# A fused convolution and feed-forward kernel: how its first block is evicted and transposed, and which engine copies the weights' exchanged halves

## The chip, the cores and the metric

The kernel runs on one core of a Trainium2 chip. The metric is the device time of one execution in microseconds (us); less is better. The median of three runs before the change is 536.28 us (536.27 to 536.34).

A core has a matrix engine (PE, with its weight loads shown as PEld), a vector engine (DVE), a scalar engine (ACT), a general engine that also issues the casting loads (POOL, GpSimd) and a queue engine for other transfers (SP). PE writes its results to PSUM. Here PSUM is used as four slots of two banks each, handed out in rotation under one tag, "banks".

## The reference

```python
w = softmax(weight, axis=-1)                     # 8 heads x 7 taps
x_pad = concatenate([zeros(B, 6, D), x], axis=1) # B, S, D = 8, 3904, 192
out[b, s, h, g] = sum_k w[h, k] * x_pad[b, s + k, h, g]   # 8 heads of 24 channels
x = out.reshape(31232, 192)
a = x @ w1                                       # 192 -> 1024
b = x @ w2                                       # 192 -> 1024
return ((a * b) @ w3) @ w_out                    # 1024 -> 1024 -> 192
```

## The kernel before, in words

**Two streams.** The 31232 tokens are cut into two halves (streams r = 0 and 1) of 15616 tokens that are worked on together. The partitions 64r to 64r+63 belong to stream r wherever an operand has 64 channels in 128 partitions.

**Convolution.** A window is 64 tokens, of which 58 give results. Windows are grouped in blocks of 10, 8, 10, 18, 16, 20, 36 ... windows (`SIZES`). `load_x` loads a block's windows as bf16; `conv(b, h0, nh)` (L240 to L269) multiplies them with a small band matrix per head (`Aband`, L203 to L224, made from the taps) into the PSUM tile `cps`, and L266 evicts that to the block's tile `convo`, in pieces of at most 64 channels. The channel groups k = 0, 1, 2 are channels 0 to 63, 64 to 127 and 128 to 191; four heads are 96 channels, so the first half of a block fills group 0 and half of group 1 and the second half the rest.

**Transposes.** The products want channels on partitions. For the first three blocks `pe_transposes` (L298 to L313) does it on PE: all groups go to one PSUM tile `tps` (five transposes each for block 0), and L311 copies each group to `xT[k]`, a ring of 2048 tokens. Later blocks go through DRAM (`store`, `transposes`).

**Products.** `first_product(R)` (L339 to L362) handles 512 tokens of each stream. For each of eight column groups ft of 128 columns it makes `pa` (x @ w1) and `pb` (x @ w2): six matmuls each, in pairs r = 0, 1 over k = 0, 1, 2. ACT evicts `pa` to `asb` (L358), DVE multiplies `asb` with `pb` into `abT` (L359). `second_product` (L364) multiplies `abT` with `W_sb` = w3 @ w_out, which is itself made during the first rounds by `fold` (w3 is transposed on PE at L401 and multiplied at L410).

**The weights' exchanged halves.** A matmul of stream r contracts over the 64 partitions 64r to 64r+63, so both streams need each weight on both halves of the partitions. `wn[0]` holds w1's channels 0 to 127, `wn[1]` those of w2, and `wn[2]` holds w1's channels 128 to 191 in partitions 0 to 63 and w2's in partitions 64 to 127. `wsw[k]` is `wn[k]` with its two halves of 64 partitions exchanged. `swap_w` (L328 to L331) makes it with two copies, one for each half, and the column half (512 columns) is an argument; the list of engines names who does which copy. `w_of` (L323) says which tile a matmul takes: `pa` needs `wsw[0]` and one half of `wsw[2]`, `pb` needs `wsw[1]` and the other half of `wsw[2]`. A column group ft needs the columns 128 ft to 128 ft + 127.

**Order of the work.** It is written out by hand: each engine does its instructions in the order of the program. Around the change that order is: warm-up matmuls on zeros (`warm`, L175 to L178: five, then the matmul that spreads the taps, then seven), the band, `load_x(1)`, the two convolutions of block 0 with evictions by (ACT, DVE) and (DVE, ACT), its 15 transposes, the copies to `xT` (DVE, ACT, DVE) with the exchange of `wsw[0]`'s columns 0 to 511 after the first, then the other exchanges of these columns, then `wsw[0]`'s upper columns by POOL. The other upper columns are exchanged inside the first product: `wsw[2]` after ft 1 and `wsw[1]` after ft 2, where the later loads are issued too. `first_product` takes a table of such insertions, done after the ft of their key: the blocks 1 and 2 are convolved and transposed there.

**POOL's loads.** POOL issues the loads in program order: block 0, the eight pieces of the weights, block 1, block 2, w_out, w3. In the trace they use eight semaphores in turn (104 to 111), and a load waits, before it is issued, for the landing of the load eight places ahead of it.

Of the kernel before, what the change touches and what calls it, by code (L numbers as in the profile page):

```python
# [16 lines left out]
def kernel(  # L17
# [10 lines left out]
    nc = tc.nc  # L28
# [4 lines left out]
    DFF = moe_w1.shape[1]  # L33
# [10 lines left out]
    ST = Q - PAD  # L44
# [4 lines left out]
    SIZES = [10, 8, 10, 18, 16, 20] + [36] * 5 + [10]  # L49
# [5 lines left out]
    def tok(i):  # L55
        return (i // WB) * S + (i % WB) * ST
# [8 lines left out]
    def banks(name):  # L65
        return psum.tile([128, NS, CH], FP32, tag="banks", name=name)

    def banks_bf16(name):
        return psum.tile([128, 16, 128], BF16, tag="banks", name=name)
# [7 lines left out]
    def halves_of(b):  # L77
        n = SIZES[b] // 2
        return [(FIRST[b], 2 * n)] if 2 * n <= MAXN else [(FIRST[b], n), (FIRST[b] + n, n)]
# [4 lines left out]
    def x_spans(r, i, m):  # L84
        return bass.AP(tensor=x.tensor, offset=(r * TS + tok(i) - PAD) * D,
                       ap=[[D, Q], [ST * D, m], [1, D]])

    def load_x(b, parts=(0, 1)):
        tiles = xb_of.setdefault(b, [])
        zeros_of = zero_rows.setdefault(b, [])  # L90
        for i0, n in [v for e, v in enumerate(halves_of(b)) if e in parts]:
            xb = work.tile([128, n, D], BF16, tag="xb", bufs=6, name="xb")
            w = 0
            if i0 == 0:
                nc.vector.memset(xb[:, 0, :], 0.0)
                for r in range(NS):
                    nc.gpsimd.dma_start(out=xb[Q * r:Q * r + Q, 1:n, :], in_=x_spans(r, 1, n - 1))  # L97
                w = n
            while w < n:
                i = i0 + w  # L100
                m = min(n - w, WB - i % WB)
                at_end = i + m == NWIN
                if at_end:
                    m -= 1
                if m:
                    for r in range(NS):
                        nc.gpsimd.dma_start(out=xb[Q * r:Q * r + Q, w:w + m, :],  # L107
                                            in_=x_spans(r, i, m))
                if i % WB == 0:
                    zeros_of += [(xb, 0, w), (xb, 1, w)]  # L110
                w += m
                if at_end:
                    nc.gpsimd.memset(xb[Q:128, w, :], 0.0)
                    t = tok(NWIN - 1) - PAD
                    nc.gpsimd.dma_start(out=xb[0:Q, w, :], in_=x_rows[t:t + Q, :])
                    nc.gpsimd.dma_start(out=xb[Q:Q + PAD + LAST, w, :],
                                        in_=x_rows[TS + t:TS + t + PAD + LAST, :])
                    w += 1
            if len(halves_of(b)) == 1:
                tiles += [(xb, 0), (xb, SIZES[b] // 2)]  # L120
            else:
                tiles.append((xb, 0))
# [13 lines left out]
    for r in range(NS):  # L136
        ps = slice(Q * r, Q * r + Q)
        nc.gpsimd.affine_select(
            out=diag[ps], in_=diag[ps], pattern=[[-1, Q + K - 1]], compare_op=ALU.is_equal,
# [11 lines left out]
    ident = const.tile([128, 128], BF16)  # L151
# [11 lines left out]
    HC = DFF // 2  # L163
# [11 lines left out]
    def warm(n):  # L175
        t = banks("warm")
        for j in range(n):
            nc.tensor.matmul(t[:, j % 2, :], zeros[:, 0:128], zeros, start=True, stop=True)  # L178

    warm(5)  # L180

    low = const.tile([H, 1], FP32)
    total = const.tile([H, 1], FP32)
# [5 lines left out]
        out=share, in0=taps.unsqueeze(1).to_broadcast([H, H, K]), scalar=total,  # L189
# [5 lines left out]
    for r in range(NS):  # L195
        ps = slice(Q * r, Q * r + Q)
        nc.vector.tensor_copy(
            out=wsb[ps],
            in_=spread[ps, 0, 0:H * K].rearrange("p (g a e k) -> p g a e k", g=2, a=2, e=2)
                [:, :, r].unsqueeze(4).to_broadcast([Q, 2, 2, K, 2]))  # L200
    warm(7)

    Aband = const.tile([128, 2, 2, 2, Q], BF16)  # L203

    def band_of(h, r):
        g, j, e = h // 4, (h % 4) // 2, h % 2
        return Aband[Q * r:Q * r + Q, g, int(j != r), e, :]
# [3 lines left out]
        out=cprod.rearrange("p h k (s two) -> p h k s two", two=2),  # L211
# [15 lines left out]
    xT = [const.tile([128, RING], BF16, name=f"xT{k}", tag=f"xT{k}") for k in range(NP)]  # L227

    convo_of = {}
    wt = {}  # L230

    def segments(c0, n):
        out = []
        while n:
            m = min(n, Q - c0 % Q)
            out.append((c0 // Q, c0 % Q, m))
            c0, n = c0 + m, n - m
        return out

    def conv(b, h0, nh, evict=None):  # L240
        n = SIZES[b] // 2
        if h0 == 0:
            convo_of[b] = work.tile([128, n, NP, NS, Q], BF16, tag="convo", bufs=2, name="convo")
        convo = convo_of[b]
        cps = banks("cps")
        wd = nh * G

        def view(ps, r):
            return cps[ps, r, 0:n * wd].rearrange("p (w g) -> p w g", g=wd)

        for j in range(nh):
            h = h0 + j
            for c in range(2):
                xb, w0 = xb_of[b][c]
                for r in range(NS):
                    nc.tensor.matmul(  # L256
                        view(slice(Q * c, Q * c + Q), r)[:, :, j * G:(j + 1) * G],
                        band_of(h, r),
                        xb[Q * r:Q * r + Q, w0:w0 + n, h * G:(h + 1) * G],
                        start=True, stop=True)  # L260
        src = cps[:, :, 0:n * wd].rearrange("p r (w g) -> p r w g", g=wd)
        o = 0
        for e, (k, c0, m) in enumerate(segments(h0 * G, wd)):
            dst = convo[:, :, k, :, c0:c0 + m].rearrange("p w r g -> p r w g")
            f = evict or [nc.scalar.copy]
            f[e % len(f)](out=dst, in_=src[:, :, :, o:o + m])  # L266
            o += m
        if h0 + nh == H:
            del xb_of[b]  # L269
# [25 lines left out]
                    nc.sync.dma_start(out=dst[s0:s1], in_=src[s0:s1])  # L295
                w += m

    def pe_transposes(b, after_first=None):  # L298
        n = SIZES[b] // 2
        convo = convo_of[b]  # L300
        tps = banks_bf16("tps")
        for k in range(NP):
            for w in range(n):
                nc.tensor.transpose(  # L304
                    out=tps[:, k * n + w, :],
                    in_=convo[:, w, k].rearrange("p r g -> p (r g)"), identity=ident)
        t0 = tok(FIRST[b])
        for k in range(NP):
            dst = xT[k][:, t0:t0 + 2 * n * ST].rearrange("p (c w s) -> p c w s", c=2, w=n)
            src = tps[:, k * n:(k + 1) * n, :].rearrange("p w (c s) -> p c w s", c=2)  # L310
            (nc.scalar.copy if k == 1 else nc.vector.tensor_copy)(out=dst, in_=src[:, :, :, 0:ST])  # L311
            if k == 0 and after_first:
                after_first()  # L313

    def transposes(R, first=0):
        t0, t1 = max(R * CH, first), min((R + 1) * CH, TS)
# [8 lines left out]
            return (wn if i == r else wsw)[2]  # L325
        return (wn if k == r else wsw)[i]

    def swap_w(k, half, engines):  # L328
        cs = slice(half * HC, (half + 1) * HC)
        for f, (d, e) in zip(engines, ((0, Q), (Q, 0))):  # L330
            f(out=wsw[k][d:d + Q, cs], in_=wn[k][e:e + Q, cs])  # L331

# [57 lines left out]
    def load_wo():  # L390
        nc.gpsimd.dma_start(out=wo_b, in_=wor)

    def load_w3(jt):
        w3b_of[jt] = stage.tile([128, DFF], BF16, tag="w3b", bufs=JT, name="w3b")
        nc.gpsimd.dma_start(out=w3b_of[jt], in_=w3r[:, jt, :])
# [19 lines left out]
    V, A, P = nc.vector.tensor_copy, nc.scalar.copy, nc.gpsimd.tensor_copy  # L415

    load_x(1)
    conv(0, 0, 4, evict=(A, V))
    conv(0, 4, 4, evict=(V, A))
    pe_transposes(0, lambda: swap_w(0, 0, (V, V)))  # L420
    swap_w(2, 0, (A, V))
    swap_w(1, 0, (A, V))
    swap_w(0, 1, (P, P))
    def seq(*fs):
        def run():
            for f, *a in fs:
                f(*a)
        return run
# [5 lines left out]
            w3_product(jt - 1)  # L434

    def later_loads():
        swap_w(1, 1, (P, V))
        load_x(2)
        load_wo()
        for jt in range(4):  # L440
            load_w3(jt)
        load_x(3)
        for jt in range(4, JT):
            load_w3(jt)
        for b in (4, 5, 6):
            load_x(b)

    first_product(0, {
        1: seq((swap_w, 2, 1, (V, A))),
        2: later_loads,  # L450
        4: seq((conv, 1, 0, 4)),
        5: seq((conv, 1, 4, 4)),
        6: seq((pe_transposes, 1)),
        7: seq((conv, 2, 0, 4))})
    first_product(1, {
        0: seq((conv, 2, 4, 4)),
        1: seq((fold, 0)),
        2: seq((pe_transposes, 2), (store, 2, 26)),
        3: seq((fold, 1)),
        5: seq((fold, 2)),  # L460
# [85 lines left out]
```

## Time and profile before

| | |
|---|---|
| median of three runs | 536.28 us |
| the profiled execution | 535.81 us |
| its span, first to last instruction | 534.1 us |
| PE busy | 523.2 us, 98% |
| DVE busy | 350.5 us, 66% |
| ACT busy | 324.0 us, 61% |
| POOL busy | 47.9 us, 9% |
| mean granted clock of PE | 0.994 |

All times of views are counted from the span's start. A line of the timeline gives start, duration, engine, line of the program, operation, tiles written and read, shape and count, and in brackets how long the engine had been idle and what released it. The stretches' table gives busy time per engine in a stretch, with the number of instructions, then the granted clock as a share of full speed. The chain of waits is followed back from the last instruction. In the trace six matmuls of a `pa` or `pb` take 0.65 us at full clock (six starts from 16.99 to 17.64 us) and twice that at half clock (13.99 to 15.28 us).

### The profile page before, as it was taken

Reading aid. Unit: us, or ns where it says so; the run is one execution under the profiler, and the core shown is the slowest. Engines: PE = TensorE matmul, PEld = TensorE weight load, DVE = VectorE, ACT = ScalarE, POOL = GpSimd, SP = SyncE. Lnnn points to the kernel's source line nnn. Section 1 sums busy time; section 2 is a strip of 40 time slices with the busy share of each in tenths; the row PEclk is TensorE's granted clock in tenths of the full one; section 3 lists DMA queues with packets and bytes.
Section 4 is the critical chain, followed back from the end, with each engine's and each line's share of the span. In section 5 each row is a group of like instructions: output and inputs, shape, how many; then the busy total and the mean of one; then the engine's idle time right before and its main releaser. Section 6 shows DMA issues by size and latency. Waiting matters only on the chain.

```text
span 534.1 us, 12779 instructions
## 1 busy us (share of the span) xinstructions
PE 523.2 (98%) x5495; PEld 345.9 (65%) x5495; DVE 350.5 (66%) x339; ACT 324.0 (61%) x368; POOL 47.9 (9%) x85
## 2 busy tenths in 40 slices
PE   6999999999999999999999999999999999999996
PEld 2445675766758567585675857658576684856676
DVE  6667639578394884939749396593956929377470
ACT  3766557566474665737657375573756647475562
POOL 8641001001010010200101010020000000000000
PEclk8899999999999999999999999999999999999999
DMA  8999568765489455974659656593316543130304
GB/s 112 165 201 192 94 141 159 125 167 68 136 154 139 119 67 155 139 148 101 83 159 146 135 90 98 156 149 112 68 35 186 79 136 75 60 104 14 108 1 149
DMA packets 130459, 63.10 MB, mean 118 GB/s; under 512 B 83270, under 2 KB 129378, under 8 KB 130402
## 3 DMA queue, kind: packets, MB, share of 16 engines
q1 hardware_dynamic: 91842, 45.65, 35.5%
q0 software_dynamic: 38544, 16.63, 25.7%
q8 instruction: 43, 0.70, 0.5%
q14 instruction: 14, 0.11, 0.1%
q10 hardware_dynamic: 16, 0.00, 0.0%
HBM read 33.25 MB, written 34.82 MB: 127 GB/s over the span
## 4 chain that ended last, share of the span: by engine, by line
PE 93%; DVE 2%; ACT 2%; DMA 1%; issue 1%; POOL 0%; ACTq 0%; POOLq 0%
PE ops L370 31%; PE pa L352 29%; PE pb L352 29%; PE cps L256 3%; DVE abT L359 2%; ACT asb L358 2%; PE wps L410 1%; DMA xb<-in_x_dram 1%; PE w3ps L401 1%; POOL xb L97 0%; DVE ws L331 0%; PE tps L304 0%; ACT convo L266 0%; DVE xT L311 0%; DVE convo L266 0%
## 5 line engine op out<-in xcount | busy, mean ns | idle before, releaser
L359 DVE TENSOR_TENSOR abT<-asb,pb 128x1024 bf16<-128x1024 bf16 (+1 forms) x248 | 298.1, 1203 | 56.2 <-ACT asb L358 38.8
L358 ACT CAST asb<-pa 128x1024 bf16<-128x1024 f32 (+1 forms) x248 | 247.6, 999 | 71.5 <-PE pa L352 70.8
L352 PE MATMUL pb<-xT,wn 64*128 64x512 bf16 (+1 forms) x744 | 202.6, 374 | 0.5
L352 PE MATMUL pa<-xT,wn 64*128 64x512 bf16 (+1 forms) x744 | 198.7, 374 | 1.3 <-DVE xT L311 1.0
L352 PE MATMUL pa<-xT,ws 64*128 64x512 bf16 (+1 forms) x744 | 198.7, 375 | 0.6 <-DVE ws L331 0.6
L352 PE MATMUL pb<-xT,ws 64*128 64x512 bf16 (+1 forms) x744 | 194.1, 374 | 0.0
L352 PEld LDWEIGHTS <-wn 64*128 64x128 bf16 x1488 | 137.4, 94 | 81.0 <-issue 6.3
L352 PEld LDWEIGHTS <-ws 64*128 64x128 bf16 x1488 | 128.2, 94 | 72.1 <-issue 4.8
L370 PE MATMUL ops<-W_sb,abT 128*128 128x192 bf16 x1952 | 166.3, 246 | 0.0
L370 PEld LDWEIGHTS <-abT 128*128 128x128 bf16 x1952 | 159.6, 98 | 9.9 <-issue 9.5
L375 ACT COPY osb<-ops 128x768 f32<-128x768 f32 (+1 forms) x62 | 48.9, 788 | 117.0 <-PE ops L370 117.0
L266 DVE CAST convo<-cps 128x864 bf16<-128x864 f32 (+10 forms) x47 | 38.3, 850 | 105.8 <-PE cps L256 104.1
L107 POOL DMA_DIRECT2D xb<-in_x_dram x36 | 28.8, 808 | 12.7 <-DMA xb<-in_x_dram 4.3
L499 POOL COPY pace<-abT 1x2 bf16<-1x2 bf16 x9 | 1.6, 174 | 269.9 <-DVE abT L359 269.9
L266 ACT CAST convo<-cps 128x864 bf16<-128x864 f32 (+9 forms) x39 | 22.3, 611 | 2.3 <-PE cps L256 1.4
L256 PE MATMUL cps<-xb,Aband 64*64 64x432 bf16 (+5 forms) x384 | 18.1, 285 | 1.3 <-DMA xb<-in_x_dram 1.0
L256 PEld LDWEIGHTS <-Aband 64*64 64x64 bf16 x384 | 6.9, 105 | 9.3 <-issue 7.7
L410 PE MATMUL wps<-wo_b,w3T 128*128 128x192 bf16 x64 | 6.6, 246 | 0.3 <-DVE xT L311 0.3
L178 PE MATMUL warm<-zeros 128*128 128x512 bf16 x12 | 4.9, 576 | 1.3 <-DVE zeros L142 1.3
L401 PEld LDWEIGHTS <-w3b 128*128 128x128 bf16 x64 | 3.9, 97 | 3.4 <-issue 3.0
L412 ACT CAST W_sb<-wps 128x192 bf16<-128x192 f32 x8 | 2.6, 319 | 5.8 <-PE wps L410 5.8
L410 PEld LDWEIGHTS <-w3T 128*128 128x128 bf16 x64 | 5.2, 98 | 0.9 <-issue 0.5
(50 smaller groups left out, 53.7 us busy)
## 6 DMA issues: line engine op xcount, KB each, us to landing
out_dram<-osb SPq DMA_DIRECT2D x60, 384.0 KB
xb<-in_x_dram POOLq DMA_DIRECT2D x20, 432.0 KB, 7.4
rows<-convo SPq DMA_DIRECT2D x8, 648.0 KB
w3b<-in_moe_w_dram POOLq DMA_DIRECT2D x8, 256.0 KB, 10.9
xb<-in_x_dram POOLq DMA_DIRECT2D x4, 336.0 KB, 9.7
xT<-rows SPq DMA_TRANSPOSE x84
rows<-convo SPq DMA_DIRECT2D x8, 135.0 KB
xb<-in_x_dram POOLq DMA_DIRECT2D x4, 216.0 KB, 4.4
```

The source lines that it names most:

```text
L107: nc.gpsimd.dma_start(out=xb[Q * r:Q * r + Q, w:w + m, :], in_=x_spans(r, i, m))
L178: nc.tensor.matmul(t[:, j % 2, :], zeros[:, 0:128], zeros, start=True, stop=True)
L256: nc.tensor.matmul(view(slice(Q * c, Q * c + Q), r)[:, :, j * G:(j + 1) * G], band_of(h, r), xb[Q * r:Q * r + Q, w0:w0 + n, h * G:(h + 1) ...
L266: f[e % len(f)](out=dst, in_=src[:, :, :, o:o + m])
L352: nc.tensor.matmul(p[:, r, 0:N], w_of(i, k, r)[rs, ft * 128:(ft + 1) * 128], xT[k][rs, r0:r0 + N], start=(k == 0), stop=(k == NP - 1))
L358: nc.scalar.copy(out=asb[:, :, 0:N], in_=pa[:, :, 0:N])
L359: nc.vector.tensor_tensor(out=ab[:, ft, :, 0:N], in0=asb[:, :, 0:N], in1=pb[:, :, 0:N], op=ALU.mult)
L370: nc.tensor.matmul(ops[:, g // 2, (g % 2) * D:(g % 2) * D + D], ab[:, jt, r, g * 128:(g + 1) * 128], W_sb[:, jt, :], start=(jt == 0), stop ...
L375: nc.scalar.copy(out=osb.rearrange("p (a g) d -> p a (g d)", g=2), in_=ops[:, 0:ng // 2, 0:2 * D])
L401: nc.tensor.transpose(out=tps[:, gt, :], in_=w3b[:, gt * 128:(gt + 1) * 128], identity=ident)
L410: nc.tensor.matmul(wps[:, 0, 0:D], w3T[:, gt, :], wo_b[:, gt, :], start=(gt == 0), stop=(gt == JT - 1))
L412: nc.scalar.copy(out=W_sb[:, jt, :], in_=wps[:, 0, 0:D])
```

## The change

Four things change, all at the start of the kernel:

- block 0's first convolution tile is evicted by ACT alone, its second by DVE alone;
- block 0's transposes go to one PSUM tile for each channel group, and ACT, DVE, DVE copy them to `xT`; DVE's exchange copies for `wsw[0]` stand in DVE's order before its first copy to `xT`;
- `swap_w` takes a range of columns. Columns 0 to 255 of the exchanged halves are made before the first product (k = 0 by DVE twice, k = 2 by ACT twice, k = 1 by DVE and ACT), columns 256 to 511 after ft 0 by DVE and ACT, columns 512 to 1023 all by POOL, in the order k = 0, 2, 1. POOL's order is now block 1, block 2, six copies, w_out, four pieces of w3, block 3;
- the warm-up has six and eight matmuls in the place of five and seven, and two more come between block 0's convolution and its transposes.

```diff
-    warm(5)
+    warm(6)
...
-    warm(7)
+    warm(8)
...
+    def first_transposes(between):
+        n = SIZES[0] // 2
+        convo = convo_of[0]
+        for k, f in enumerate((nc.scalar.copy, nc.vector.tensor_copy, nc.vector.tensor_copy)):
+            tps = banks_bf16("tps")
+            for w in range(n):
+                nc.tensor.transpose(
+                    out=tps[:, w, :],
+                    in_=convo[:, w, k].rearrange("p r g -> p (r g)"), identity=ident)
+            if k == 1:
+                between()
+            f(out=xT[k][:, 0:2 * n * ST].rearrange("p (c w s) -> p c w s", c=2, w=n),
+              in_=tps[:, 0:n, :].rearrange("p w (c s) -> p c w s", c=2)[:, :, :, 0:ST])
...
-    def swap_w(k, half, engines):
-        cs = slice(half * HC, (half + 1) * HC)
+    def swap_w(k, lo, hi, engines):
+        cs = slice(lo, hi)
         for f, (d, e) in zip(engines, ((0, Q), (Q, 0))):
             f(out=wsw[k][d:d + Q, cs], in_=wn[k][e:e + Q, cs])
...
     load_x(1)
-    conv(0, 0, 4, evict=(A, V))
-    conv(0, 4, 4, evict=(V, A))
-    pe_transposes(0, lambda: swap_w(0, 0, (V, V)))
-    swap_w(2, 0, (A, V))
-    swap_w(1, 0, (A, V))
-    swap_w(0, 1, (P, P))
+    load_x(2)
+    for k in (0, 2, 1):
+        swap_w(k, HC, DFF, (P, P))
+    load_wo()
+    for jt in range(4):
+        load_w3(jt)
+    conv(0, 0, 4, evict=(A,))
+    conv(0, 4, 4, evict=(V,))
+    warm(2)
+    first_transposes(lambda: swap_w(0, 0, 256, (V, V)))
+    swap_w(2, 0, 256, (A, A))
+    swap_w(1, 0, 256, (V, A))
...
     def later_loads():
-        swap_w(1, 1, (P, V))
-        load_x(2)
-        load_wo()
-        for jt in range(4):
-            load_w3(jt)
         load_x(3)
...
     first_product(0, {
-        1: seq((swap_w, 2, 1, (V, A))),
+        0: seq(*[(swap_w, k, 256, HC, (V, A)) for k in (0, 2, 1)]),
         2: later_loads,
```

## The prediction, made before the changed kernel was run

> **What bounds the kernel now.** First the page: how busy is the engine that could be the bound?
>
> ```profile
> PE 523.2 (98%) x5495; PEld 345.9 (65%) x5495; DVE 350.5 (66%) x339; ACT 324.0 (61%) x368; POOL 47.9 (9%) x85
> ...
> PEclk8899999999999999999999999999999999999999
> ```
>
> PE is the bound (98%, and nines in the last line's tenths of granted clock), and the clock is short only in the first slices. PE's starts show no gap over 0.2 us between 40 and 510 us, so what it gains before 40 us moves the end, and nothing else does. The change lies in 1 to 22 us. The timeline there:
>
> ```profile
> 8.24 0.69 ACT L266 CAST convo<-cps 128x640 bf16<-128x640 f32 x1 [0.80 <-PE cps L256]
> ...
> 8.97 0.89 DVE L266 CAST convo<-cps 128x320 bf16<-128x320 f32 x2 [1.71 <-ACT convo L266]
> ...
> 9.89 0.69 ACT L266 CAST convo<-cps 128x640 bf16<-128x640 f32 x1 [0.95 <-DVE convo L266]
> ...
> 11.39 0.46 DVE L311 COPY xT<-tps 128x580 bf16<-128x580 bf16 x1 [1.53 <-PE tps L304]
> 11.67 1.99 POOL L331 COPY ws<-wn 64x512 bf16<-64x512 bf16 x3 [1.15 <-DMA wn<-in_moe_w_dram]
> 11.77 1.30 DVE L331 COPY ws<-wn 64x512 bf16<-64x512 bf16 x2
> ```
>
> The evictions follow one another (ACT, DVE, DVE, ACT) to 10.58; no copy to `xT` begins until all 15 transposes are done; then DVE's two exchange copies take 0.65 us each beside POOL's, and PE streams products only from 13.13. Next the granted clock, in stretches of 3.41 us, the distance at which its records change here (5.87, 9.29, 16.11):
>
> ```profile
> 5.87:9.29 3.42, 1.82 (x40) 0.97 (x38) 1.61 (x5) 1.09 (x2) 2.92 (x7) 1.00 1.10 142
> 9.29:12.70 3.41, 2.19 (x14) 1.00 (x11) 1.86 (x5) 1.48 (x3) 2.22 (x4) 0.50 1.09 152
> 12.70:16.11 3.41, 2.98 (x15) 1.11 (x17) 1.45 (x5) 2.00 (x3) 3.28 (x6) 0.50 0.89 95
> 16.11:19.52 3.41, 3.41 (x34) 1.87 (x32) 2.66 (x4) 2.74 (x4) 3.41 (x6) 1.00 1.48 167
> 528.06:531.47 3.41, 1.80 (x22) 1.57 (x20) 0.00 (x0) 0.96 (x2) 0.00 (x0) 1.00 0.58 190
> ```
>
> The first number behind the length is PE's busy time, the third from the end the clock: the first products run at half. Last the chain of waits, to see where the start hands over to the rest:
>
> ```profile
> 20.71 0.29 DVE ws L331
> ...
> 21.02 1.23 DVE abT L359
> ...
> 22.30 0.84 PE pa L352 x6
> ```
>
> So ft 5's `pa` at 22.30 waited for the product of ft 3, and before it for an exchange copy. I measure the change by when this `pa` starts.
>
> **Warm-up, front.** One matmul more ahead of the taps' spread ends at 3.81 (starts every 0.427 from 1.27); the spread started at 3.83. Cost 0 to 0.1; I take 0.1. The eight end near 6.65, before the convolution at 7.59, which waited for its load: free. The two after it take 2 x 0.215 from 8.26 and hide under ACT's first eviction (to 8.93).
>
> **Evictions.** Per row: ACT 0.69 for 640 columns, 0.46 for 320; DVE 0.82 for 640 (a row elsewhere in the trace), 0.49 for 320. ACT: 8.24, 8.93, 9.38. DVE, no longer behind ACT: 8.45 to 9.70. Before, both were done at 10.58.
>
> **Transposes and `xT`.** Group 0: 8.99 to 9.28 as before, result 9.47; ACT copies it (0.64) by 10.14. Group 1 starts when ACT's second piece is there, 9.42, group 2 at 9.75, five at 0.056 each at full clock. DVE exchanges `wsw[0]` 9.72 to 10.15 (two 64x256 copies; the same form at L224 took 0.22; POOL issues loads until 11.95 and a DVE copy beside an issue took 0.29, its price alone), then `xT[1]` to 10.61, `xT[2]` to 11.09 (0.46 each). ACT's two `wsw[2]` copies (0.40 by L223) end at 10.95, its `wsw[1]` copy, for which the load landed at 10.81, at 11.35.
>
> **First products.** Pairs of `pa` at 10.2, 10.65, 11.12; `pb` from 11.4; ft 0 ends at 12.05 at full clock, against 15.28 before. With the clock at half until 12.70: 12.85.
>
> **The copies after ft 0.** The first `asb` ends at 12.6; then ACT does three copies (1.2) before the second `asb`, 13.8 to 14.8. DVE's first product ends at 13.84, then three copies. Alone 3 x 0.22. But POOL's six copies, queued behind block 2's loads, run from 11.95 at the spacing shown (1.99 / 3) to 15.9, and the rows of this line show what that does to DVE:
>
> ```profile
> L331 DVE COPY ws<-wn x6: 281/288/660, 11.8 to 20.7; 64x512 bf16<-64x512 bf16 x6
> L331 POOL COPY ws<-wn x3: 604/606/610, 11.7 to 13.1; 64x512 bf16<-64x512 bf16 x3
> ```
>
> 0.28 alone, 0.63 to 0.66 beside POOL. So the three cost 0.66 to 1.9, and I take 1.7 (the first finds POOL in mid-copy), nearest to the contended rows. Then the products: 15.55 to 16.77, and two more at the 1.13 spacing of two in a row (2.35 for two): the third after it ends at 19.03. On PE, ft 2's `pb` waits for the last (15.6), ft 3's for the slot of ft 1's product (16.8), ft 4 ends at 18.75, block 1's convolution at 19.05 (its load landed at 15.0), and ft 5's `pa` starts at **19.1 in place of 22.30: 3.2 us**. With DVE's copies alone it would be 18.45: 3.85.
>
> **What goes away later.** The exchange copies after ft 1 and 2 (DVE 0.29 each, ACT 0.62), for which PE waited at 19.05 and 21.05. POOL's copies end at 15.9, ft 4 needs them at 17.5.
>
> **POOL's queue.** Block 2's loads are issued 3.1 us earlier, w_out and w3 0.8 later (15.9 against 15.11). The first piece of w3 landed at 24.0 and was used at 32.1; 24.8 against 29.0 leaves 4 us. Block 3 landed at 33.4 and is used at 46.3. Nothing waits.
>
> **The clock.** 5.87 to 9.29 lost it with 1.82 us busy; 528.06 to 531.47 kept it with 1.80, so busy time does not tell. Columns over clock do: 1.28 us (38%) against 20 x 0.0825 (46%, at least 1.57). The change adds an eighth matmul (0.24) and two (0.43): 1.95, 57%. I take it that the clock stays. The Trainium skill ("TensorE: Matmul & The Clock Gate", Part 1) says the clock falls after an idle window of some 3.4 us; the stretch that lost it here was 38% streaming, so the trace disagrees, and by that rule the extra matmuls would be unneeded and the sum the same. The same section calls the window free-running, which speaks against three extra matmuls holding it in every run; the three runs of before within 0.07 us show no such shift, and that rule gives the first rival below.
>
> **Sum.** 3.2 less 0.1 is 3.1 us: the profiled execution from 535.81 to 532.7. The median is 0.47 above the profiled execution, which I keep: 536.28 - 3.1 = **533.2**.
>
> **Rivals.**
> - The clock falls at 9.29 all the same (38 and 46% are only one stretch each). ft 0 ends at 12.85, `asb` at 13.0, DVE's copies at 16.05, `pa` of ft 5 at 19.55 or so: gain 2.6, **533.7**. Chance 0.18.
> - DVE is not held by POOL after ft 0: gain 3.75, **532.5**. The rows above speak against it. Chance 0.11.
> - The clock falls later, at 16.11, after a stretch in which PE waits for exchanges (about 57% streaming by my times). ft 3 then takes 2.6, ft 5 starts at 20.7: gain 1.6, **534.7**. Stretches down to 73% kept it. Chance 0.09.
> - It doesn't do what it says: ACT's and DVE's evictions still follow one another because both write `convo`. `xT[2]` is 0.6 later: **533.8**. Group 0's transposes at 8.99 ran while DVE wrote group 1 of the same tile, which speaks against it. Chance 0.05.
> - The lead is given back before 40 us, where PE waited 2.8 us in all for ACT, DVE and their slots: within 1 us of before, say **536**. It needs a fixed time in that stretch, such as w3's first piece 4 to 7 us later than I count. Chance 0.08.
> - **Slower**: POOL's six copies become the bound. All upper columns hang on them, and DVE's copies hold them as they hold DVE. Ft 4 needs the last. At 0.66 us each they are done at 15.9; at 0.93, 17.5, they begin to cost; from (21.05 - 11.95) / 6 = 1.5 us each all is lost, and at 1.7 the time is **537.4**. Only three rows, all near 0.606, speak against it. Chance 0.09.
>
> **Numbers.** The forecast has 0.40. A measurement can tell about 0.2% (1.07 us) from no change: faster by more, 0.40 + 0.18 + 0.11 + 0.09 + 0.05 = 0.83; same 0.08; slower 0.09. The range runs from 532.2 (copies alone, no spread delay) to 535.0 (the clock lost at 16.11) and leaves out 0.17.
>
> **What the new profile would show.** DVE's first eviction at 8.45; `xT[0]` by ACT at 9.5; first `pa` at 10.2 and ft 0's `pb` over by 12.1; a granted clock of 1.00 from 5.87 on; DVE's three copies after the first product at 0.2 to 0.65 each; POOL's six copies 11.95 to 15.9; ft 5's `pa` at 19.1; from there the trace of before moved by 3.1. Wrong would be a clock of 0.50 at 10 us, a POOL copy over 0.9, or a wait of PE for w3 or `xb`.

## The result, and the profile after

The changed kernel takes **532.1 us** (median of four runs, 532.07 to 532.46) against 536.27 us (four runs) measured beside it: ratio 0.9925 [0.9907, 0.9942], so faster, by less than 1%. The profiled execution went from 535.81 to 532.46 us, 3.35 less; its span from 534.1 to 530.7. A second measurement on another chip (changed_again below) gave 532.45 (531.98 to 532.87, five runs) against 535.87 (17 runs): 3.4 less, 0.9937 [0.9924, 0.9951]. Over three chips the kernel before had medians of 535.76, 535.87 and 535.85. So the first difference, 4.2 us, may be large by the scatter of a few runs on both sides; I take the gain as about 3.4 us, against the 3.1 of the prediction. The first median, 532.1, lies just below the predicted range (532.2 to 535.0), and at its edge as a ratio (0.9925, where 532.2 of 536.28 is 0.9924); the second, 532.45, lies inside.

The page of the changed kernel, the two lines that answer to those of before:

```profile
PE 522.3 (98%) x5499; PEld 344.8 (65%) x5499; DVE 350.3 (66%) x339; ACT 324.1 (61%) x371; POOL 49.8 (9%) x88
...
PEclk9999999999999999999999999999999999999999
```

PE is still the bound and is no less busy, but the eights at the start of the clock's line are gone. The timeline of the changed kernel where block 0 is evicted and transposed:

```profile
8.09 1.02 ACT L266 CAST convo<-cps 128x640 bf16<-128x640 f32 x2 [0.50 <-PE cps L256]
...
8.30 1.22 DVE L266 CAST convo<-cps 128x320 bf16<-128x320 f32 x2 [0.89 <-PE cps L256]
...
9.32 0.64 ACT L324 COPY xT<-tps 128x580 bf16<-128x580 bf16 x1 [0.22 <-PE tps L319]
9.44 0.45 DVE L343 COPY ws<-wn 64x256 bf16<-64x256 bf16 x2
9.91 0.83 DVE L324 COPY xT<-tps 128x580 bf16<-128x580 bf16 x2
...
10.02 0.37 PE L364 MATMUL pa<-xT,wn 64*128 64x512 bf16 x1
```

Both engines evict from the moment PE frees their tile, the second no longer released by the first. The first copy to `xT` begins at 9.32, as soon as group 0's own five transposes are done, and no longer at 11.39 after all fifteen; the first `pa` streams at 10.02. The stretches of the granted clock, at the changed kernel's own bounds (its record of the clock begins at 5.74, when the clock rises to full):

```profile
5.74:9.15 3.41, 2.72 (x44) 1.25 (x42) 2.38 (x7) 1.42 (x3) 3.33 (x7) 1.00 1.17 152
9.15:12.56 3.41, 3.17 (x28) 1.35 (x27) 1.77 (x6) 2.58 (x5) 2.62 (x5) 1.00 0.99 136
12.56:15.98 3.42, 3.13 (x29) 1.16 (x27) 3.04 (x5) 3.16 (x6) 3.16 (x6) 1.00 1.54 184
```

The clock (third from the end) is 1.00 throughout; in before it was 0.50 in the second and third stretch. Last the chain of waits of the changed kernel, from the start to ft 2:

```profile
5.97 5.41 DMA wn<-in_moe_w_dram
...
11.40 0.40 ACT ws L343
...
11.83 1.02 ACT asb L370
...
12.87 1.16 DVE abT L371
...
14.13 0.31 DVE ws L343
...
14.48 0.61 PE pa L364 x4
```

The evictions are gone from the chain. In their place stands the landing of w2's first load (`wn[1]`, 5.97 + 5.41 = 11.38): ACT's exchange copy of it ends at 11.81, the first `asb` stands behind it on ACT, and `pb` of ft 0 waits for the same load. Ft 0 is over at 12.31 (15.28 before) and ft 5's `pa` starts at **18.79 in place of 22.30**. From 45 us on the trace is that of before moved by 3.4 to 3.5 us: the lead is kept.

### The profile page after: what moved, and what is told of

The parts are those of the page before. It is cut to its first block, busy times and chain, and to the rows that moved or that the text cites. A ratio compares the mean times of both kernels' runs of the same rounds, so it can differ in the third digit from the quotient of the medians.

```text
span 530.7 us, 12794 instructions
## 1 busy us (share of the span) xinstructions
PE 522.3 (98%) x5499; PEld 344.8 (65%) x5499; DVE 350.3 (66%) x339; ACT 324.1 (61%) x371; POOL 49.8 (9%) x88
## 4 chain that ended last, share of the span: by engine, by line
PE 93%; ACT 2%; DVE 2%; DMA 1%; POOL 1%; issue 0%; ACTq 0%; POOLq 0%
PE ops L382 31%; PE pa L364 29%; PE pb L364 29%; PE cps L256 3%; DVE abT L371 2%; ACT asb L370 1%; DMA wn<-in_moe_w_dram 1%; PE wps L422 1%; PE w3ps L413 1%; POOL xb L97 0%; POOL xb L128 0%; ACT convo L266 0%; DVE xT L311 0%; POOL wn L167 0%; POOL wn L168 0%
## 5 line engine op out<-in xcount | busy, mean ns | idle before, releaser
L178 PE MATMUL warm<-zeros 128*128 128x512 bf16 x16 | 6.0, 531 | 1.3 <-DVE zeros L142 1.3
## 6 DMA issues: line engine op xcount, KB each, us to landing
w3b<-in_moe_w_dram POOLq DMA_DIRECT2D x8, 256.0 KB, 10.2
```

## The experiments

**Theory one** is the prediction's: PE's start is earlier because evictions, transposes and copies overlap, and the added warm-up matmuls keep the clock up. Its **rivals**: the clock stays up for another reason (the earlier products fill the stretch), or the gain sits in the smaller and earlier exchange copies. The kernel before measured 535.76, 535.87 or 535.85 us beside these runs, according to the chip.

**no_extra_warm**: the changed kernel without the three added matmuls.

```diff
-    warm(6)
+    warm(5)
...
-    warm(8)
+    warm(7)
...
-    warm(2)
```

> The changed kernel with the warm-up of before: five and seven matmuls, and none between block 0's convolution and its transposes. Theory one (the extra matmuls hold the clock): the stretch from about 5.8 to 9.2 us is some 40% streaming as before, the granted clock falls to 0.50 near 9.2 and rises near 12.6, PE ends the first ft about 0.6 us later, and the time is 532.6 to 532.8, 0.5 to 0.7 above the changed kernel. Rival (the clock would have held anyway, or half clock is hidden under the copies that PE waits for): no row below 1.00 after 5.8 us, or ft 5's pa still at 18.8, and 532.1 within 0.2.

Measured 532.41 us (531.96 to 532.99), 0.9938 [0.9926, 0.995], the time of the changed kernel. The mean clock was 0.999 to 1.000 in all five runs. The stretches of its profiled execution:

```profile
4.46:7.87 3.41, 2.02 (x36) 0.92 (x37) 2.63 (x6) 0.40 (x1) 3.41 (x7) 1.00 1.46 185
7.87:11.28 3.41, 2.73 (x40) 1.30 (x28) 2.73 (x6) 2.47 (x5) 2.86 (x5) 1.00 0.87 114
11.28:14.69 3.41, 3.06 (x26) 1.12 (x26) 2.04 (x5) 3.25 (x6) 2.86 (x5) 1.00 1.43 181
```

Theory one's warm-up part fell: the clock holds without them, and ft 5's `pa` starts at 18.74, as the rival has it. The stretches also begin at another moment than in the runs above (4.46, not 5.87 or 5.74).

**warm_only**: before, with only the three matmuls added.

```diff
-    warm(5)
+    warm(6)
...
-    warm(7)
+    warm(8)
...
     conv(0, 4, 4, evict=(V, A))
+    warm(2)
```

> The kernel before with the changed warm-up alone (six, eight, and two behind block 0's convolution). Theory one: the clock holds at 9.2, but the next stretch (9.2 to 12.6) is only about 30% streaming, since evictions, transposes and exchange copies follow one another as before; the clock then falls at 12.6 and PE's products from 13.13 run at half as before: 536.0 to 536.4, no change. Rival (once kept the clock stays): ft 0 at full clock from 13.13, pa of ft 5 about 1 us earlier, 535.0 to 535.4.

Measured 535.57 us (534.06 to 536.4, twelve runs), 0.9995 [0.9986, 1.0003]: no difference, with a median 0.4 under the range expected for it. The spread is the finding. Its runs order themselves by mean granted clock: 534.06 and 534.71 at 1.000, 535.12 to 535.84 at 0.997, 535.69 to 536.08 at 0.995 and 0.996, 536.4 at 0.993. One stretch of 3.41 us at half clock takes 0.0032 off the mean of 534 us, so the ends are none and two lost stretches, and 0.997 is one. (This mean counts only what lies behind the first record of the clock. The half clock of the very start, which differs from run to run, is not in it.) The 45 runs of before all lost one or two: 17 at about 0.997 (medians 535.4 to 535.5), 28 at 0.992 to 0.994 (535.9 to 536.0). The added matmuls alone save the clock in a few executions and not in most.

**evict_only**: before, with the one-engine evictions and a tile for each group, and nothing else (`first_transposes` is added as in the change).

```diff
...
-    conv(0, 0, 4, evict=(A, V))
-    conv(0, 4, 4, evict=(V, A))
-    pe_transposes(0, lambda: swap_w(0, 0, (V, V)))
+    conv(0, 0, 4, evict=(A,))
+    conv(0, 4, 4, evict=(V,))
+    first_transposes(lambda: swap_w(0, 0, (V, V)))
```

> The kernel before with the evictions by one engine each and the transposes in a tile per channel group, and nothing else: columns 0 to 511 exchanged before the first product as before, upper columns as before, warm-up as before. Theory one (the serial evictions and the single transpose tile were most of it): the first product starts near 10.5, the clock falls at 9.2 and rises near 12.6, ft 5's pa starts at 19.0 to 19.6, and the time is 532.8 to 533.6. Rival (the split of the exchange copies carries half of the gain, since 512 columns by DVE and ACT hold the first product up): 534.2 or more.

Measured 532.87 us (532.27 to 533.2), 0.9941 [0.9928, 0.9953]: 2.9 of the 3.4 us, at a clock of 0.999 to 1.000 in every run. Its chain:

```profile
11.90 1.25 PE pb L366 x6
...
17.82 0.46 DVE ws L345
18.31 1.23 DVE abT L373
19.58 0.84 PE pa L366 x6
```

`pb` starts 0.5 later than in the changed kernel, because w2's load landed 0.5 later in this execution (11.86). Ft 5's `pa`, at 19.58, still waits behind an exchange copy (17.82) and is 0.8 later than there, of which that landing can be 0.5. By the medians the other exchange order and the matmuls add 0.4 us to this part, and the two intervals overlap: a small share, not settled.

**swaps_and_warm**: the changed kernel with before's evictions and single transpose tile (`pe_transposes` as in before).

```diff
...
-    conv(0, 0, 4, evict=(A,))
-    conv(0, 4, 4, evict=(V,))
+    conv(0, 0, 4, evict=(A, V))
+    conv(0, 4, 4, evict=(V, A))
     warm(2)
-    first_transposes(lambda: swap_w(0, 0, 256, (V, V)))
+    pe_transposes(0, lambda: swap_w(0, 0, 256, (V, V)))
```

> The changed kernel with evictions (ACT, DVE; DVE, ACT) and the one transpose tile of before; exchange copies by 256 columns, POOL's six copies and the warm-up as changed. Theory one: the first product starts near 11.9, the clock falls at 12.6 after a stretch of about 30% streaming and rises at 16, ft 5's pa at about 20.9, 534.6 to 535.2. Rival (the exchange copies were the main brake): 533.3 or less.

Measured 534.4 us (533.98 to 535.1, seven runs), 0.9976 [0.9966, 0.9987]: 1.4 us of gain, 0.2 under the range expected. Ft 5's `pa` starts at 20.81 (expected 20.9). Four of the seven runs, at a clock of 0.995 and 0.996, took 534.4 to 535.1; the three at 0.998 to 1.000 took 533.98 to 534.31. The profiled execution loses the clock in spite of the added matmuls:

```profile
5.07:8.48 3.41, 2.47 (x41) 1.08 (x39) 2.20 (x5) 0.80 (x2) 3.34 (x7) 1.00 1.35 160
8.48:11.89 3.41, 2.07 (x19) 0.98 (x18) 1.70 (x5) 1.41 (x3) 2.48 (x5) 1.00 1.02 146
11.89:15.31 3.42, 3.42 (x16) 1.30 (x18) 1.30 (x3) 2.96 (x7) 3.16 (x6) 0.50 1.50 179
```

The bounds fell so that the waits of the evictions and of the first products lie in one stretch. Its PE was "busy" for 2.07 us, but streamed columns for 35% of it, and the next one ran at 0.50. The two matmuls behind the convolution lie in the stretch before, which is 58% streaming.

**one_engine_evictions** and **tile_per_group**: each half of that part alone, on before. The first:

```diff
...
-    conv(0, 0, 4, evict=(A, V))
-    conv(0, 4, 4, evict=(V, A))
+    conv(0, 0, 4, evict=(A,))
+    conv(0, 4, 4, evict=(V,))
```

> The kernel before with the first convolution tile evicted by ACT alone and the second by DVE alone, and nothing else (one transpose tile, exchange copies and warm-up as before). Theory one (behind the evictions the next limit is the landing of the w2 load near 11.4 to 11.9 and the 512-column copies that follow it, so that each half of the edit gives nearly all of what both give): transposes done near 10.0, ft 0 over near 13.1, 532.9 to 533.3, no more than 0.4 above evictions and transposes together (532.87). Rival (the gains of the halves add): some 1.5 us of gain alone, 534.2 to 534.6.

Measured 533.63 us (533.24 to 535.23, seven runs), 0.9965 [0.9953, 0.9977]. Ft 0 was over at 13.18 and ft 5's `pa` started at 20.01. Theory one's figure was missed by some 0.3, as the seven runs include two at a clock of 0.997, with 534.3 and 534.4, and one at 0.993, with 535.23; with the clock at 0.998 to 1.000 it is 533.24 to 533.63. The second (`first_transposes` is added as in the change):

```diff
...
-    pe_transposes(0, lambda: swap_w(0, 0, (V, V)))
+    first_transposes(lambda: swap_w(0, 0, (V, V)))
```

> The kernel before with the transposes in a tile per channel group and the copies to xT by ACT, DVE, DVE, and nothing else (evictions by ACT, DVE, DVE, ACT as before). Theory one (as for the evictions alone): ACT's copy to xT waits behind its last eviction to 10.45, first product near 11.1, ft 0 over near 13.0 if the clock holds, 533.0 to 533.7. Rival (the gains of the halves add, and this half is the smaller): 535 or more.

Measured 533.49 us (532.55 to 533.96), 0.9955 [0.9942, 0.9967]; ft 5's `pa` at 19.04 in the execution that kept the clock (532.55; the four at 0.997 took 533.4 to 533.96). So the halves bring 2.2 and 2.4 us alone and 2.9 together. They don't add. The traces show what was late next. In the first, w2's load landed at 12.05, and `pb` of ft 0 waited for it and for the copies behind it. In the second it had landed at 10.98, and PE waited to 11.75 for DVE's exchange copy of 512 columns. The clock plays its part too: the one run of tile_per_group that kept it, 532.55, lies in the range of both halves together.

**changed_again**: the changed kernel, unaltered, beside other kernels on one chip.

> The changed kernel once more, as the base for the others on this chip: 532.1, within 0.4. Theory (the granted clock's stretches begin at another moment in each execution, and the changed kernel has no stretch under 46% streaming after its start): every run at a mean clock of 0.999 or 1.000, while the runs before scatter with the clock between 0.992 and 0.997 and about 1.5 us apart. Rival (the clock plays no part in the difference): the runs before scatter without regard to their clock.

Measured 532.45 us, as told above. Its profile shows how far one execution differs from the next: w2's load landed at 10.63 in place of 11.38, but DVE's three copies after ft 0 took longer and ft 5's `pa` started at 18.71, nearly the same. DVE's row there:

```profile
13.74 1.30 DVE L343 COPY ws<-wn 64x256 bf16<-64x256 bf16 x3
```

In the first profile of the changed kernel the same row reads:

```profile
14.13 0.99 DVE L343 COPY ws<-wn 64x256 bf16<-64x256 bf16 x3
```

**pool_twice**: the changed kernel with each of POOL's copies made twice (twelve in the place of six), to price the slower rival.

```diff
-    for k in (0, 2, 1):
+    for k in (0, 0, 2, 2, 1, 1):
         swap_w(k, HC, DFF, (P, P))
```

> The changed kernel with each of POOL's six copies of the upper columns done twice in a row, twelve in all: the suspected cost of the slower rival doubled. By the prediction's working the copies are done near 20.3 in place of 16.3, the exchanged w2 half last; ft 4's pb, at 17.7, waits for it to 20.3, and the time rises by 2.2 to 2.6 us, to 534.3 to 534.8. Rival (ft 4 has more slack than the working says, or the loads behind POOL's copies, issued 3.9 us later, hurt as well): under 533.3, or over 535.3.

Measured 536.33 us (534.75 to 536.89, eight runs), 1.0009 [0.9998, 1.0019]: the whole gain is gone. POOL's row, PE's row at the wait, and the stretches:

```profile
11.96 7.98 POOL L343 COPY ws<-wn 64x512 bf16<-64x512 bf16 x12
```

```profile
20.00 0.61 PE L364 MATMUL pb<-xT,ws 64*128 64x512 bf16 x2 [2.24 <-POOL ws L343]
```

```profile
16.48:19.89 3.41, 1.27 (x11) 0.41 (x7) 1.91 (x2) 1.68 (x2) 3.12 (x7) 1.00 0.21 23
19.89:23.30 3.41, 3.30 (x29) 1.20 (x31) 1.22 (x1) 0.86 (x2) 3.41 (x7) 0.50 0.62 60
```

The copies end at 19.94 and PE waits for the last one, as the expectation's theory has it (to 20.3). The one run that kept its clock took 534.75, the stall alone, inside the 534.3 to 534.8 of that theory. The other seven, at 0.995 to 0.997, took 536.06 to 536.89, which is over the rival's bound: in the profiled one the stretch behind the stall runs at half clock, after the stall left the one before it 33% streaming. The theory had left that out. The mechanism of the prediction's slower rival is real; in the changed kernel it is some 1.4 us away (the copies are over at 16.35, and `pb` of ft 4, which needs the last, starts at 17.71).

Four kernels looked for a better version or priced what was left. **early_exchange** makes DVE's three copies of columns 256 to 511 before the first product instead of after it (an engine given as `None` makes no copy).

```diff
...
     swap_w(1, 0, 256, (V, A))
+    for k in (0, 2, 1):
+        swap_w(k, 256, HC, (V,))
...
-        0: seq(*[(swap_w, k, 256, HC, (V, A)) for k in (0, 2, 1)]),
+        0: seq(*[(swap_w, k, 256, HC, (None, A)) for k in (0, 2, 1)]),
```

> The changed kernel with DVE's three exchange copies of columns 256 to 511 moved from after its first product to before it, into the time in which DVE is idle (11.3 to 12.5); ACT's three stay. Theory (those copies, held up by POOL's, are what PE waits for in ft 2: 0.45 to 1.0 us at 14.4): that wait is gone, the second product starts near 14.5 in place of 15.1, ft 5's pa at about 18.2, 531.9 or less, 0.3 to 0.6 under the changed kernel (532.45 on the chip before). Rival (ACT's second asb and the slots then set the pace): within 0.2 of it.

Measured 532.27 us (531.73 to 532.54), 0.9933 [0.992, 0.9945], not to be told from the changed kernel's 532.1 and 532.45. DVE's rows:

```profile
11.38 0.64 DVE L344 COPY ws<-wn 64x256 bf16<-64x256 bf16 x4
12.88 1.22 DVE L372 TENSOR_TENSOR abT<-asb,pb 128x1024 bf16<-128x1024 bf16 x1 [0.86 <-ACT asb L371]
14.96 3.48 DVE L372 TENSOR_TENSOR abT<-asb,pb 128x1024 bf16<-128x1024 bf16 x3 [0.86 <-ACT asb L371]
```

The wait in ft 2 is gone, but DVE then idles 0.86 for the second `asb`, which stands behind ACT's three copies, and PE waits 0.6 at 16.23 instead. Ft 5's `pa` starts at 18.58, 0.2 earlier than in the changed kernel, though the first `pa` came 0.5 later in this execution (10.53). The limit moved from DVE to ACT, as the rival has it; a gain beyond 0.2 us is not shown.

**weights_split** loads columns 0 to 255 of the weights first, then 256 to 1023 (`load_w` takes a range of columns).

```diff
...
-    load_w(0)
-    load_w(1)
+    load_w(0, 256)
+    load_w(256, DFF)
```

> The changed kernel with the weights loaded as columns 0 to 255 and then 256 to 1023, in place of two halves of 512: eight loads in the same order. Theory (the first pb waits for the landing of w2's piece, at 10.6 to 11.4, and POOL's second load of block 2 with it): that piece lands near 9.5, the first pb starts near 11.1 in every execution and POOL's copies near 11.7; but ft 2 still waits for the exchange copies, so little is gained, 532.2 to 532.6. Rival (the later pieces, three times as large, land too late for the copies of columns 256 to 511): 533 or more.

Measured 532.68 us (532.23 to 532.81), 0.9941 [0.9928, 0.9953]: nothing gained, and 0.1 over what was expected. Its chain:

```profile
8.13 5.68 DMA wn<-in_moe_w_dram
...
13.84 0.40 ACT ws L343
...
14.26 1.02 ACT asb L370
```

w2's first piece lands at 8.49, so the wait of `pb` is gone, but the larger second piece lands at 13.81 and holds ACT's third copy and the second `asb` behind it. **split_and_early** adds to this the early copy of `wsw[0]`.

```diff
...
     swap_w(1, 0, 256, (V, A))
+    swap_w(0, 256, HC, (V,))
...
+        0: seq(*[(swap_w, k, 256, HC, (None if k == 0 else V, A)) for k in (0, 2, 1)]),
```

> The changed kernel with the split loads of the run before and, of DVE's copies of columns 256 to 511, the first (for wsw[0]) moved before the first product. Theory: both waits are gone, 531.5 to 532.0. Rival (the copy now waits for the larger load and holds DVE's first product): 532.4 or more.

Measured 532.82 us (532.51 to 533.31), 0.9945 [0.9932, 0.9959]: the second piece landed at 13.95 and held ACT's third copy again (13.97), not DVE's early one (11.03). No version clearly beats the changed kernel.

**no_warmup**: the changed kernel without any warm-up matmul.

```diff
-    warm(6)
...
-    warm(8)
...
-    warm(2)
```

> The changed kernel with no warm-up matmul at all: the price of a cold start. Theory (the clock rises at the end of the first stretch of 3.41 us that is over some 40% streaming, wherever the stretches lie): half clock until 11 to 15 us, the first two column groups' 24 matmuls at half, 532.8 to 534.0 and a wide scatter, mean clock 0.98. Rival (PE waits for copies and loads there anyhow): within 0.3 of the changed kernel.

Measured 533.06 us (532.62 to 533.38), 0.9948 [0.9936, 0.9961], 0.6 above changed_again, which ran on another chip, and the two ranges overlap. The profiled execution ran at half clock to 12.70 and started ft 5's `pa` at 19.38. Its mean clock is still listed as 0.999 to 1.000, not the expected 0.98, since the start before the first record is not counted. All sixteen warm-up matmuls together are worth some 0.6 us here.

## Why the prediction was right, and where it was not

- **Evictions and first products: right.** DVE's evictions 8.30 to 9.52 (forecast 8.45 to 9.70), `xT[0]` at 9.32 (9.5), first `pa` at 10.02 (10.2); the 0.15 to 0.2 between them are the convolution's start, 7.64 in place of 7.80, since block 0's last load landed earlier in this execution (7.28, against 7.67). evict_only shows that this part carries 2.9 of the 3.4 us.
- **Ft 0 over at 12.05: 0.26 too early.** I took w2's landing as fixed at 10.81. It landed at 11.38, and between 10.42 and 12.05 in the twelve profiles with this load. With the evictions out of the way, this landing sets `pb` and the first `asb`.
- **DVE's three copies, mis-sized.** I took 1.7 us; they took 0.99, and 1.30 in changed_again. In the first profile only the last was held for the whole of one of POOL's copies (0.63; the others took 0.30 and 0.22), in changed_again two were (0.61 and 0.64). That 0.4 to 0.7 is why the second product began at 15.15, not 15.55, and `pa` of ft 5 at 18.79, not 19.1. The bounds, 0.66 and 1.9, held.
- **POOL's copies: right in size, late in start.** They ran 12.43 to 16.35 at 0.60 to 0.63 each (forecast 11.95 to 15.9): block 2's second load waited for w2's landing before it was issued. Ft 4 did not wait for them. w3's first piece landed at 22.7 and was used at 28.6, so POOL's longer queue cost nothing, as forecast.
- **The median: 0.8 us by a term that did not carry over.** The sum kept the 0.47 us by which the three runs of before lay above the profiled execution. In the result the median lies 0.36 below the profiled one (532.1 and 532.46). Of the 1.1 us between 533.2 and 532.1 that is 0.8; the path itself, 532.7 against 532.46, was off by 0.25. By the gain, 3.4 us, the result is midway between the forecast's 3.1 and the second rival's 3.75, and DVE's copies took neither 1.7 us nor 0.66.
- **The clock stays at 1.00: right in the outcome, wrong in the reason.** The step that failed is "I take it that the clock stays", worked out from 38 and 46% with the added matmuls bringing 57% in the stretch 5.87 to 9.29, and with the close runs of before as evidence that the stretches do not shift. (The 46% is 1.57 to 1.59 us; 20 x 0.0825, as written there, would be 1.65 or 48%.) They do shift: the first change of the clock came at 3.99, 4.46, 5.07, 5.87, 6.24 and 7.72 in executions whose start is the same or within one matmul, and at 5.74 and 4.64 in two of the same kernel. That the three runs of before lay within 0.07 us says little: all 45 runs of before with a clock on record lose one or two stretches, and the medians of these two groups are only some 0.5 us apart. no_extra_warm and evict_only kept the clock in all ten runs without the matmuls, swaps_and_warm lost it in four of seven with them. The reading that fits is that the clock holds where no stretch of 3.41 us, however placed, has too little streaming in it. It is inferred, as each profile shows one placing. The Trainium skill's rule ("TensorE: Matmul & The Clock Gate", Part 1) that the window is free-running agrees with these runs. The Trainium skill's other rule there, that the clock falls after an idle window, does not: it fell after stretches of 33, 35 and 38% streaming.
- **The 0.1 for the warm-up ahead of the taps: right in size, but lost behind a load.** The last step of `Aband` began 0.14 later (6.86 against 6.72). In the changed kernel's profile the convolution waited for it (ACT's part ended at 7.59, the load had landed at 7.28), and the first `pa` starts at 10.02; in no_extra_warm it is 9.88. Ft 0 is over at 12.31 and 12.27, because `pb` waits for w2's load in both (landed at 11.38 and 11.34).
- **How the gain divides.** With the clock held, the kernel before (with three matmuls more) takes 534.06 and 534.71, and the changed kernel 532.07 to 532.87. So by this estimate about 2 us come from the earlier start and about 1.4 from stretches no longer lost. It rests on two runs. The prediction had both in its 3.2, since before's profile shows two lost stretches.
- **Rivals.** None of the falling clocks (at 9.29, at 16.11) came about: the changed kernel's mean clock was 0.998 or more in nine of nine runs, and one lost stretch would be 0.0032. "Still one after the other" fell with DVE's eviction at 8.30, and "lead given back" with the trace after 45 us. "DVE not held by POOL" was half true. The slower rival was priced by pool_twice at 4 us when POOL's copies double; I had all lost from 1.5 us each. At its 1.33 each (two copies of 0.665) the stall alone left 1.1 us of the gain, near to what the rival's figures give (nothing lost at 0.93, all 3.1 us at 1.5); with the clock that such a stall loses, which I had not counted, nothing was left.

## What to carry to other kernels

At a kernel's start, look for the worst placing of a clock stretch, not the one that the profile shows: slide 3.41 us over PE's columns and see where they are thinnest; closing a wait there can pay twice, in the wait and in the clock. Here two engines that evict one tile each beat two engines that share both; the reader's first transposes need only one of the tiles. Don't expect the halves of such a change to add: each exposes what is late next. After removing a wait, list the loads that land just behind it: their scatter (1.6 us over twelve profiles here) becomes yours.

## What the runs showed of the hardware that was not expected

- **The clock's threshold.** A matmul counts here as streaming for the time that its columns take by the starts in the traces (512 columns in 0.215 us at full clock, 0.427 at half), and matmuls that start together count once. Of the stretches at full clock, those with 33 (pool_twice), 35 (swaps_and_warm) and 38% (before) lost it for the next stretch; those with 41 (tile_per_group), 42 (one_engine_evictions), 46 (before, at its end) and 48% (no_extra_warm) kept it. Each figure is one stretch. PE's busy time of the profile does not order them: 2.07 us lost it, 2.02 kept it. At half clock more of the time has to be filled: before's stretch 9.29 to 12.70 streamed for 42% and the clock stayed at half, while it rose after some 76% (warm_only, to 3.99) and 78% (no_extra_warm, to 4.46). If the stretches are counted back from the first rise, it also stayed after 68% (evict_only, to 4.20) and 71% (one_engine_evictions, to 4.31). In columns, 76% at half clock is as much as 38% at full.
- **DVE's copies end just behind POOL's.** In the changed kernel two of DVE's 64x256 copies that ran beside one of POOL's ended 0.08 us after it (14.42 after 14.345, 15.115 after 15.035); the one between them, which began as POOL's copy ended, took 0.22. In before the two 64x512 copies ended 0.15 after POOL's (12.426 after 12.278, 13.069 after 12.924). The 0.07 between is what 256 more columns cost when nothing interferes (0.22 and 0.29 us). So it looks as if all of a copy's columns were moved after POOL's end, and only its fixed part before. POOL's own copy went from 0.61 to 0.63. The Trainium skill ("SBUF — State Buffer", Who interferes with whom) describes an exclusive lock, held for a whole instruction, with the other engine blocked. The traces agree, for a DVE copy that finds POOL's under way.
- **A DVE copy beside POOL's issue of a load may take twice as long.** I priced DVE's copies of `wsw[0]` alone beside an issue, at 0.22; that held in the changed kernel's first profile (0.45 for two), but the second copy took 0.45 in changed_again, 0.55 in no_extra_warm and in pool_twice and 0.51 in weights_split, each time while POOL issued block 1's second load. It was issuing it in the changed kernel's first profile too, so what decides it is left open.
